# Two attention blocks on one core: the keys' feature map as a power of e on GpSimd

## The chip, the core and the metric

The kernel runs on one core of a Trainium2 chip. The core has TensorE (PE, matmuls), VectorE (DVE), ScalarE (ACT), GpSimd (POOL), and a queue on SyncE (SP) that issues most DMAs. Each engine works through its own list of instructions in order; semaphores tie the lists together. The metric is the device time of one launch in microseconds, as the median of several runs.

## The reference

Two attention blocks, A and B, stand side by side; their outputs are concatenated. Both have a sequence of 2048, a width of 1024 and 32 heads of 32. A is ordinary softmax attention. B goes through four segments of 512 positions. In each it computes causal softmax attention inside the segment and mixes it, by a gate per head, with what it reads from a memory that the earlier segments have written.

```python
phi = lambda t: jnp.where(t > 0, t + 1.0, jnp.exp(t))
for s in range(N):                      # N = 4 segments
    logits = einsum('bhqd,bhkd->bhqk', qs, ks) * scale + mask
    a_dot = einsum('bhqk,bhkd->bhqd', softmax(logits), vs)
    pq = phi(qs)
    num = einsum('bhld,bhde->bhle', pq, M)
    den = einsum('bhld,bhd->bhl', pq, z)[..., None] + 1e-06
    o = g * (num / den) + (1.0 - g) * a_dot
    pk = phi(ks)
    M = M + einsum('bhld,bhle->bhde', pk, vs)
    z = z + pk summed over the segment
```

The feature map phi is what the change is about. It is needed for the keys in segments 0, 1 and 2 (the memory written in the last segment is never read), and for the queries in segments 1, 2 and 3 (the memory is empty in the first).

## The kernel before

The heads are worked on in eight groups of four (4 x 32 = 128 partitions). A's attention is cut into chunks of 256 queries; B's into units, one for each segment s and group j. Both give the same stream: TensorE computes a block of scores into PSUM, ScalarE takes its exponential in pieces of up to 1536 columns (L772) and writes it as P, and TensorE multiplies P with V (L821) and with ones (L827, the softmax's denominator). Where a piece of B lies on the diagonal, GpSimd masks P with an affine_select (L784) before TensorE may use it. VectorE divides and stores. Two sets of three PSUM banks alternate between TensorE and ScalarE, so TensorE can be at most one block of scores ahead.

Everything else is filled in around that stream: projections of keys, queries and values (L449; results are copied out of PSUM by VectorE, L971, L1140 and L1153), output projections (L1250), and B's memory. All of these jobs share one PSUM bank (`X_BANKS`). After each key or query projection GpSimd squares the result (`square`, L977); the squares give a bound on the scores, which is the bias of the exponential.

The order of instructions on every engine is fixed when the program is built. The class `Prog` holds a list of operations, each with an engine, a planned duration, a key (roughly the planned time at which it is wanted) and its reads and writes. `schedule` plays the engines forward with these planned durations. Whenever an engine is free, it takes, among the operations whose inputs are ready, the one with the smallest key; an operation is not held back until its key. TensorE has a rule of its own (`pick`) that puts blocks of scores first and jobs in the gaps. On the chip the engines then follow exactly these lists. The planned durations are `n / rate / 1000 + fixed` us, with `rate` 0.96 for VectorE, 1.2 for ScalarE, 1.2 for GpSimd and 0.5 for GpSimd's squares; the fixed part is 0.12, 0.142 and 0.15 us.

B's memory has three jobs for each segment and group. `job_phi` (L1166) makes the feature map in the tile `PKQ_B`, of which there are two (`j % 2`); each has a key half (index 0) and a query half (index 1). It computes phi(t) as min(exp(t), 1) + max(t, 0): the exponential on ScalarE (L1174) for both halves in one instruction of 1024 columns where both are needed, of 512 columns otherwise; the min on VectorE in place (L1176); the max and sum on VectorE (L1179), one instruction for each half, which for the keys also adds up z. `job_mem` (L1183) reads the memory with the query half. `job_M` (L1205) takes the key halves of two groups, transposes them with eight DMAs from SP's queue (L1215) and adds their product with V to the memory. Its key is `M_AT = 14` us behind the unit's start, while `job_phi` lies in the four us ahead of that start.

The constants are set at the beginning by a chain of GpSimd instructions (`plan_constants`, L624), all of which go through one resource, `r_c`.

Of the kernel before, what the change touches and what calls it, by code (L numbers as in the profile page):

```python
# [5 lines left out]
dt = mybir.dt  # L6
ACT = mybir.ActivationFunctionType
ALU = mybir.AluOpType
AX = mybir.AxisListType

P = 128
# [6 lines left out]
L = 512  # L18
# [10 lines left out]
        (7, 6), (7, 7))  # L29
CHUNKS = [(g, c) for g in range(6) for c in range(8)] + list(PAIR)  # L30
BIAS0 = 16
B_FIRST, B_STEP, B_GAP = 9.0, 1.35, 2.5
B_STEP3 = 1.2

# [20 lines left out]
def holds(rs, *tag):  # L55
    for r in rs:
        assert r.tag == tag, (r.tag, tag)


def mark(rs, *tag):  # L60
    for r in rs:
        r.tag = tag
# [77 lines left out]
MARGIN = 1.5  # L140
# [4 lines left out]
XR = 6  # L145
XC = 0
M_AT = 14.0


class Prog:  # L150
# [266 lines left out]
class _Kernel:  # L417
# [7 lines left out]
    def sb(self, name, shape, dtype=dt.bfloat16):  # L425
        return self.es.enter_context(self.nc.sbuf_tensor(name, shape, dtype))
# [65 lines left out]
    def alloc(self):  # L492
        nc = self.nc
        sb = self.sb
# [67 lines left out]
        self.gc = sb("gc", [P, 4, 8], dt.float32)  # L562
        self.r_g = Res()
        self.warm = sb("warm", [P, 2], dt.float32)
        self.cols = sb("cols", [P, 64], dt.float32)
        self.dg = sb("dg", [P, 2, P], dt.float32)
        self.r_dg = Res()
# [56 lines left out]
    def plan_constants(self):  # L624
        c = self.r_c
        k0 = -100.0

        def pool1(f, n=128):
            self.item(k0, lambda key, f=f, n=n: self.pool(f, n, key, (c,), (c,)))
        pool1(lambda e: e.memset(self.warm[:, :], 0.0), 2)  # L630
        self.item(k0, lambda key: self.act(lambda e: e.activation(self.warm[:, :], self.warm[:, :], ACT.Exp), 1500, key,
                                           (c,), (c,)))
        pool1(lambda e: e.memset(self.identf[:, :], 0.0))
        pool1(lambda e: e.affine_select(self.identf[:, :], self.identf[:, :], pattern=[[-1, P]],
                                        compare_op=ALU.not_equal, fill=1.0, base=0, channel_multiplier=1))
        pool1(lambda e: e.memset(self.onesf[:, :], 1.0))
        pool1(lambda e: e.memset(self.onesb[:, :], 1.0), 32)

        pool1(lambda e: e.memset(self.blk32[:, :], 1.0), 32)
        for r in range(4):  # L640
            rows = slice(32 * r, 32 * r + 32)
            pool1(lambda e, rows=rows, r=r: e.affine_select(
                self.blk32[rows, :], self.blk32[rows, :], pattern=[[1, 32]], compare_op=ALU.is_ge, fill=0.0,
                base=-8 * r, channel_multiplier=0), 32)
            pool1(lambda e, rows=rows, r=r: e.affine_select(
                self.blk32[rows, :], self.blk32[rows, :], pattern=[[-1, 32]], compare_op=ALU.is_ge, fill=0.0,
                base=8 * r + 7, channel_multiplier=0), 32)
        pool1(lambda e: e.memset(self.maskbd[:, :], 1.0))
        for r in range(4):
            rows = slice(32 * r, 32 * r + 32)  # L650
            pool1(lambda e, rows=rows, r=r: e.affine_select(
                self.maskbd[rows, :], self.maskbd[rows, :], pattern=[[1, P]], compare_op=ALU.is_ge, fill=0.0,
                base=-32 * r, channel_multiplier=0))
            pool1(lambda e, rows=rows, r=r: e.affine_select(
                self.maskbd[rows, :], self.maskbd[rows, :], pattern=[[-1, P]], compare_op=ALU.is_ge, fill=0.0,
                base=32 * r + 31, channel_multiplier=0))


    def tiles_att_A(self, g, c, part=None):
# [4 lines left out]
        for t in range(lo, hi):  # L664
# [3 lines left out]
            for h in range(4):  # L668
                tiles.append(dict(unit=("A", g, c), kind="A", g=g, c=c, h=h, w=512, pieces=pieces, set=key, part=part, pv=pv,
                                  bias=BIAS0 if part == 0 else g % 2))  # L670
        return tiles
# [326 lines left out]
    def guard_A0(self, key):  # L998
        col = self.guard_cols(key, self.sqA[(0, 0)] + self.sqA[(0, 1)], 512)
        self.guard_end(key + 0.2, [self.col0, col], 2, [0], halves=True)  # L1000
        rb, r0 = self.r_bias[0], self.r_bias[BIAS0]
        x = self.act(lambda e: e.activation(self.f0[:, :], self.bias[:, BIAS0:BIAS0 + 1], ACT.Exp, bias=self.bias[:, 0:1],
                                            scale=-1.0), 1, key + 1.0, [rb, r0], [self.r_f0])
# [33 lines left out]
    def plan_prologue(self):  # L1037
# [19 lines left out]
        def half0(key):  # L1057
# [20 lines left out]
            self.col0 = self.guard_cols(key, sq, 512)  # L1078
            self.guard_end(key, [self.col0], 2, [BIAS0])
        self.item(-50.0, half0)  # L1080
# [83 lines left out]
        self.sqB.setdefault((s, j), []).append(self.square("B", dst, self.r_KQB[j][kq], key + 1.5))  # L1164

    def job_phi(self, s, j, key):  # L1166
        a, b = (0 if s < 3 else 1), (2 if s > 0 else 1)
        n = (b - a) * L
        holds(self.r_KQB[j], "KQ", s, j)
        mark(self.r_PKQ[j % 2], "P", s, j)  # L1170
        PKQ, rp = self.PKQ[j % 2], self.r_PKQ[j % 2]
        src = self.KQB[:, j, a:b, :]
        rs = [self.r_KQB[j][k] for k in range(a, b)]
        x = self.act(lambda e: e.activation(PKQ[:, a:b, :], src, ACT.Exp), n, key, rs, rp[a:b], fixed=0.19)  # L1174
        x.margin = MARGIN
        self.dve(lambda e: e.tensor_scalar(PKQ[:, a:b, :], PKQ[:, a:b, :], 1.0, None, ALU.min), n / 4, key, rp[a:b], rp[a:b])  # L1176
        for k in range(a, b):
            kw = dict(accum_out=self.zs[:, j:j + 1]) if k == 0 else {}
            self.dve(lambda e, k=k, kw=kw: e.scalar_tensor_tensor(out=PKQ[:, k, :], in0=self.KQB[:, j, k, :], scalar=0.0,  # L1179
                                                                  in1=PKQ[:, k, :], op0=ALU.max, op1=ALU.add, **kw), L,  # L1180
                     key + 0.5, [self.r_KQB[j][k], rp[k]], [rp[k]] + ([self.r_zs[j]] if k == 0 else []))

    def job_mem(self, s, j, key):  # L1183
        holds(self.r_PKQ[j % 2], "P", s, j)
# [129 lines left out]
    def plan_jobs(self):  # L1314
# [34 lines left out]
        for s in range(NSEG):  # L1349
# [31 lines left out]
            for j in range(8):  # L1381
# [4 lines left out]
                if s < 3:  # L1386
                    if j % 2 == 1:
                        self.item(SB[j] + M_AT, lambda key, s=s, j=j: self.job_M(s, j - 1, key))
        for k in range(8):
# [70 lines left out]
```

## Time and profile before

| what | value |
|---|---|
| median of 3 runs | 1219.09 us (1216.64 to 1220.8) |
| the profiled execution | 1215.55 us, of it the span 1213.8 us |
| granted TensorE clock | 0.993 |
| ScalarE, exponentials of scores (L772) | 827 instructions, 1147.0 us busy |
| ScalarE, feature map (L1174) | 16 of 1024 columns, mean 1246 ns; 16 of 512, mean 860 ns |
| VectorE, min of the feature map (L1176) | 16 of 1024, mean 502 ns; 16 of 512, mean 331 ns |
| VectorE, max and sum (L1179) | 48 of 512, mean 786 ns |
| GpSimd, squares (L977) | 124 of 512, 1046 and 1049 ns |
| GpSimd, masks (L784) | 64 of 768, mean 865 ns; 32 of 384, 552 ns; 32 of 128, 357 ns |
| SP, transposes of the feature map (L1215) | 96, median 1233 ns |

A group's mean duration is that of single instructions, and neighbours on ScalarE overlap: the 827 exponentials have a larger sum of durations than the busy time. The span is the time from the first to the last instruction; some 1.75 us of the profiled execution lie outside it.

### The profile page before, as it was taken

How to read it: one execution, taken by the hardware profiler on the slowest of the kernel's cores; microseconds unless marked ns; L12 is line 12 of the kernel's file. 1: busy time of each engine (PE TensorE's matmuls, PEld its weight loads, DVE VectorE, ACT ScalarE, POOL GpSimd, SP SyncE). 2: the span in 40 equal slices, each digit the busy share in tenths (PEclk: the TensorE clock that was granted, in tenths of full speed). 3: DMA queues.
4: the chain of work that ended last, by engine and by line, in shares of the span. 5: the costliest groups of instructions: out<-in, count | busy, mean ns of one | idle time of the engine just before them, and what ended most of it. 6: DMA issues, size and time to landing. Idle time of an engine off the chain costs nothing.

```text
span 1213.8 us, 52835 instructions
## 1 busy us (share of the span) xinstructions
PE 1128.2 (93%) x24712; PEld 544.3 (45%) x24712; DVE 550.1 (45%) x1241; ACT 1166.5 (96%) x870; POOL 216.0 (18%) x279
## 2 busy tenths in 40 slices
PE   6889999999999989998999999999999999899998
PEld 4444444464444445534444444454444444434443
DVE  1234244434352545546443555564535555543222
ACT  3879999999999999999999999999999999999995
POOL 1112131312230211122120221312102231010000
PEclk9989999999999999999999999999999999999999
DMA  9632222303111222202311122201112410001001
GB/s 177 163 78 53 76 60 46 72 20 68 39 41 39 70 49 41 68 19 53 75 24 44 39 52 47 57 25 44 55 46 63 139 33 12 24 25 33 32 29 36
DMA packets 166619, 65.67 MB, mean 54 GB/s; under 512 B 136192, under 2 KB 163584, under 8 KB 166400
## 3 DMA queue, kind: packets, MB, share of 16 engines
q1 hardware_dynamic: 164032, 61.51, 20.8%
q8 instruction: 193, 3.16, 1.1%
q10 hardware_dynamic: 2368, 0.79, 0.3%
q14 instruction: 26, 0.21, 0.1%
HBM read 39.00 MB, written 11.73 MB: 42 GB/s over the span
## 4 chain that ended last, share of the span: by engine, by line
ACT 76%; PE 15%; DVE 4%; issue 3%; SPq 1%; DMA 0%; POOL 0%; DVEq 0%; ACTq 0%
ACT P L772 75%; PE ps L449 8%; PE ps L757 3%; PE ps L821 2%; PE ps L827 2%; ACT PKQ_B L1174 1%; SPq L1050 1%; DVE T L845 1%; DVE PKQ_B L1179 1%; DMA Wv_A<-in_A_wqkv_dram 0%; DVE KQ_A L971 0%; DVE T L854 0%; DVE KQ_B L971 0%; DVE PKQ_B L1176 0%; DVE OT_B L1200 0%
## 5 line engine op out<-in xcount | busy, mean ns | idle before, releaser
L772 ACT ACTIVATE P<-ps,bias 128x1536 bf16<-128x1536 f32 (+3 forms) x827 | 1147.0, 1672 | 16.3 <-PE ps L757 13.3
L827 PE MATMUL ps<-P,onesb 128*32 128x256 bf16 (+1 forms) x4864 | 299.6, 271 | 0.0
L757 PE MATMUL ps<-KQ_A 32*128 32x256 bf16 x4096 | 276.5, 274 | 20.1 <-ACT P L772 16.9
L821 PE MATMUL ps<-P,V_A 128*32 128x256 bf16 x4096 | 259.9, 277 | 10.4 <-ACT P L772 8.9
L757 PEld LDWEIGHTS ps<-KQ_A 32*128 32x128 bf16 x4096 | 80.6, 92 | 240.1 <-ACT P L772 135.2
L449 PE MATMUL ps<-xT_A,W_A 128*32 128x512 bf16 x2048 | 146.8, 388 | 12.7 <-DMA xT_A<-in_A_x_dram 7.3
L821 PEld LDWEIGHTS ps<-P,V_A 128*32 128x32 bf16 x4096 | 109.0, 96 | 82.1 <-issue 41.1
L449 PE MATMUL ps<-xT_B,W_B 128*32 128x512 bf16 x2048 | 142.0, 381 | 4.1 <-DVE cols L994 1.4
L827 PEld LDWEIGHTS ps<-P,onesb 128*32 128x32 bf16 x4864 | 130.6, 97 | 25.7
L784 POOL TENSOR_SCALAR_AFFINE_SELECT P<-P 128x768 bf16<-128x768 bf16 (+2 forms) x128 | 81.5, 660 | 254.7 <-ACT P L772 254.6
L977 POOL TENSOR_TENSOR sqB<-KQ_B 128x512 bf16<-128x512 bf16 x64 | 67.0, 1046 | 319.6 <-DVE KQ_B L971 296.3
L977 POOL TENSOR_TENSOR sqA<-KQ_A 128x512 bf16<-128x512 bf16 x60 | 63.0, 1049 | 298.7 <-DVE KQ_A L971 218.4
L1250 DVE CAST outsb<-ps 128x512 bf16<-128x512 f32 x62 | 42.9, 691 | 144.2 <-PE ps L449 144.1
L845 DVE STREAM_TRANSPOSE T<-ps 128x256 f32<-128x256 f32 (+1 forms) x148 | 72.4, 489 | 65.7 <-PE ps L827 51.5
L971 DVE CAST KQ_B<-ps 128x512 bf16<-128x512 f32 x64 | 44.1, 690 | 124.2 <-PE ps L449 121.9
L971 DVE CAST KQ_A<-ps 128x512 bf16<-128x512 f32 x60 | 41.5, 691 | 119.8 <-PE ps L449 117.8
L449 PE MATMUL ps<-Wv_A,xT_A 128*32 128x256 bf16 x2048 | 73.4, 278 | 9.9 <-issue 6.7
L854 DVE STREAM_TRANSPOSE T<-rc 128x256 f32<-128x256 f32 (+1 forms) x152 | 73.3, 484 | 4.0
L449 PEld LDWEIGHTS ps<-xT_A,W_A 128*32 128x32 bf16 x2048 | 44.9, 97 | 64.8 <-issue 31.4
L449 PE MATMUL ps<-Wv_B,xT_B 128*32 128x512 bf16 x1024 | 70.5, 382 | 2.5 <-DVE cols L994 0.7
L449 PE MATMUL ps<-Wo_B,OT_B 128*32 128x512 bf16 x1024 | 69.6, 382 | 0.8 <-DVE KQ_B L971 0.6
L449 PEld LDWEIGHTS ps<-xT_B,W_B 128*32 128x32 bf16 x2048 | 45.5, 95 | 52.2 <-issue 24.5
(81 smaller groups left out, 744.7 us busy)
## 6 DMA issues: line engine op xcount, KB each, us to landing
Wv_B<-in_B_wv_dram SPq DMA_DIRECT2D x8, 1024.0 KB, 5.5
W_B<-in_B_wk_dram SPq DMA_DIRECT2D x32, 256.0 KB, 3.1
W_B<-in_B_wq_dram SPq DMA_DIRECT2D x32, 256.0 KB, 3.0
out_dram<-outsb SPq DMA_DIRECT2D x62, 128.0 KB, 1.9
W_A<-in_A_wqkv_dram SPq DMA_DIRECT2D x14, 256.0 KB, 3.5
ot_a_scratch<-OTst SPq DMA_DIRECT2D x51, 64.0 KB, 1.8
xT_A<-ot_a_scratch SPq DMA_DIRECT2D x6, 512.0 KB, 8.2
Wv_A<-in_A_wqkv_dram SPq DMA_DIRECT2D x4, 512.0 KB, 5.1
```

The lines of the kernel that those rows point to most:

```text
L449: ins = e.matmul(out[r], w[:, r], x, start=start, stop=stop, tile_position=(0, 32 * t), skip_group_check=True)
L757: ins = e.matmul(out, kap, qap, start=st, stop=True, tile_position=(32 * h, 0), skip_group_check=True)
L772: a = self.act(lambda e: e.activation(dst, src, ACT.Exp, bias=self.bias[:, bc:bc + 1], scale=SCALE), cols, key, res + [self.r_bias[bc]], [rP])
L784: self.pool(lambda e, v=v, pat=pat: e.affine_select(v, v, pattern=pat, compare_op=ALU.is_ge, fill=0.0, base=0, channel_multiplier=-1), (m ...
L821: ins = e.matmul(self.ps[32 * h:32 * h + 32, 512 * obk + q0:512 * obk + q0 + nq], vt[:, c0 + 32 * h:c0 + 32 * h + 32], Pt[:, b, off:off + nq],
L827: ins = e.matmul(self.ps[32 * h:32 * h + 32, lcol + q0:lcol + q0 + nq], self.onesb[:, 0:32], Pt[:, b, off:off + nq], start=False, stop=las ...
L845: self.dve(lambda e: e.transpose(T1[:, 0:n], src), n, key, rsrc, [r1])
L854: self.dve(lambda e: e.transpose(T2[:, 0:n].rearrange("p (b r) -> p b r", r=32), bc), n, key, [rr], [r2])
L971: self.dve(lambda e: e.tensor_copy(dst, out), ncol, key + 1.0, [self.bank[b]], rdst)
L977: self.pool(lambda e: e.tensor_tensor(sq[:, :], src, src, ALU.mult), 512, key, [rsrc], [rs], rate=0.5)
L1050: self.dma(lambda e, i=i, h=h: e.dma_start(self.xT[:, i, 1024 * h:1024 * h + 1024], xa[1024 * h:1024 * h + 1024, P * i:P * i + P], transpo ...
L1250: self.dve(lambda e: e.tensor_copy(ob[:, :], self.ps[:, 512 * b:512 * b + 512]), 512, key + 1.0, [self.bank[b]], [ro])
```

## The change

A constant e is kept in a new tile, `euler`, one float32 for each partition, set by one more GpSimd memset among the constants. In `job_phi` the two halves are separated. The query half stays as it was, with an exponential of 512 columns on ScalarE. The key half is now computed as e to the power of min(t, 0): VectorE takes the min of the keys with 0 (from `KQ_B` straight into `PKQ_B`), then GpSimd raises e to that power in place, in two instructions of 256 elements per partition, with e broadcast along the row. The final max and sum on VectorE is the same, but the key half's gets a key 6 us behind the job's in place of 0.5 us. The plan's duration of a power is 256 / 0.2 / 1000 + 0.15 us.

```diff
+EULER = 2.718281828459045
+POW_N, POW_RATE = 256, 0.2
...
+        self.euler = sb("euler", [P, 1], dt.float32)
...
+        pool1(lambda e: e.memset(self.euler[:, :], EULER), 1)
...
     def job_phi(self, s, j, key):
-        a, b = (0 if s < 3 else 1), (2 if s > 0 else 1)
-        n = (b - a) * L
...
-        src = self.KQB[:, j, a:b, :]
-        rs = [self.r_KQB[j][k] for k in range(a, b)]
-        x = self.act(lambda e: e.activation(PKQ[:, a:b, :], src, ACT.Exp), n, key, rs, rp[a:b], fixed=0.19)
-        x.margin = MARGIN
-        self.dve(lambda e: e.tensor_scalar(PKQ[:, a:b, :], PKQ[:, a:b, :], 1.0, None, ALU.min), n / 4, key, rp[a:b], rp[a:b])
-        for k in range(a, b):
+        src, rs = self.KQB[:, j, :, :], self.r_KQB[j]
+        if s < 3:
+            self.dve(lambda e: e.tensor_scalar(PKQ[:, 0, :], src[:, 0, :], 0.0, None, ALU.min), L / 4, key, [rs[0]], [rp[0]])
+            for h in range(0, L, POW_N):
+                u = PKQ[:, 0, h:h + POW_N]
+                base = self.euler[:, 0:1].to_broadcast([P, POW_N])
+                self.pool(lambda e, u=u, base=base: e.tensor_tensor(u, base, u, ALU.pow), POW_N, key, [rp[0], self.r_c], [rp[0]],
+                          rate=POW_RATE)
+        if s > 0:
+            x = self.act(lambda e: e.activation(PKQ[:, 1, :], src[:, 1, :], ACT.Exp), L, key, [rs[1]], [rp[1]], fixed=0.19)
+            x.margin = MARGIN
+            self.dve(lambda e: e.tensor_scalar(PKQ[:, 1, :], PKQ[:, 1, :], 1.0, None, ALU.min), L / 4, key, [rp[1]], [rp[1]])
+        for k in range(0 if s < 3 else 1, 2 if s > 0 else 1):
             kw = dict(accum_out=self.zs[:, j:j + 1]) if k == 0 else {}
...
-                     key + 0.5, [self.r_KQB[j][k], rp[k]], [rp[k]] + ([self.r_zs[j]] if k == 0 else []))
+                     key + (6.0 if k == 0 else 0.5), [rs[k], rp[k]], [rp[k]] + ([self.r_zs[j]] if k == 0 else []))
```

In the changed kernel job_phi's other lines and the jobs around it stand as they were, and so do the rule by which `schedule` orders the instructions and the planned durations of all that was there.

More of the change, by code (lines that the diff above doesn't have):

```diff
@@ L1171, in job_phi @@
         PKQ, rp = self.PKQ[j % 2], self.r_PKQ[j % 2]
-        src = self.KQB[:, j, a:b, :]
-        rs = [self.r_KQB[j][k] for k in range(a, b)]
-        x = self.act(lambda e: e.activation(PKQ[:, a:b, :], src, ACT.Exp), n, key, rs, rp[a:b], fixed=0.19)
-        x.margin = MARGIN
-        self.dve(lambda e: e.tensor_scalar(PKQ[:, a:b, :], PKQ[:, a:b, :], 1.0, None, ALU.min), n / 4, key, rp[a:b], rp[a:b])
-        for k in range(a, b):
+        src, rs = self.KQB[:, j, :, :], self.r_KQB[j]
[11 more added lines that the diff above has]
+        for k in range(0 if s < 3 else 1, 2 if s > 0 else 1):
             kw = dict(accum_out=self.zs[:, j:j + 1]) if k == 0 else {}
-            self.dve(lambda e, k=k, kw=kw: e.scalar_tensor_tensor(out=PKQ[:, k, :], in0=self.KQB[:, j, k, :], scalar=0.0,
-                                                                  in1=PKQ[:, k, :], op0=ALU.max, op1=ALU.add, **kw), L,
-                     key + 0.5, [self.r_KQB[j][k], rp[k]], [rp[k]] + ([self.r_zs[j]] if k == 0 else []))
+            self.dve(lambda e, k=k, kw=kw: e.scalar_tensor_tensor(out=PKQ[:, k, :], in0=src[:, k, :], scalar=0.0, in1=PKQ[:, k, :],
+                                                                  op0=ALU.max, op1=ALU.add, **kw), L,
+                     key + (6.0 if k == 0 else 0.5), [rs[k], rp[k]], [rp[k]] + ([self.r_zs[j]] if k == 0 else []))
     def job_mem(self, s, j, key):
```

## The prediction

> **What bounds the kernel now.** I read the page's first part, then the busy time by stretches, who ScalarE waited for, and ScalarE's timeline.
>
> ```profile
> PE 1128.2 (93%) x24712; PEld 544.3 (45%) x24712; DVE 550.1 (45%) x1241; ACT 1166.5 (96%) x870; POOL 216.0 (18%) x279
> ...
> 120.00:240.00 120.00, 114.80 (x2440) 52.61 (x2434) 49.39 (x114) 119.81 (x90) 28.10 (x31) 1.00 0.27 64
> 480.00:600.00 120.00, 111.91 (x2523) 56.62 (x2515) 67.57 (x159) 117.36 (x89) 25.61 (x32) 0.97 0.17 42
> 960.00:1080.00 120.00, 110.28 (x2326) 50.79 (x2330) 65.83 (x152) 120.00 (x92) 20.88 (x28) 1.00 0.14 43
> ...
> ACT P L772 <- PE ps L757: 13.3, 11, 6.1
> ACT KQ_A L1075 <- PE ps L449: 13.1, 1, 13.1
> ACT outsb L1252 <- PE ps L449: 10.7, 2, 7.8
> ```
>
> In the stretches the columns after the length are PE, PEld, DVE, ACT and POOL. ScalarE is busy 956.2 of the 960 us from 120 to 1080 us (eight stretches, three shown), so only 3.8 us are idle there; its other idle time lies in the start and the last output rows. TensorE is busy 904.1 of the same 960 us: 56 us free. ScalarE sets the end, and TensorE is a close second. The end should therefore move with ScalarE's work until something makes TensorE late.
>
> **What the change takes from ScalarE.** The duration of a ScalarE row is not its price, because one instruction starts before the last has drained. The price is the step from its start to the next start:
>
> ```profile
> 235.26 0.88 ACT L1174 ACTIVATE PKQ_B<-KQ_B 128x512 bf16<-128x512 bf16 x1
> 235.78 4.65 ACT L772 ACTIVATE P<-ps,bias 128x1536 bf16<-128x1536 f32 x3
> ...
> 422.09 1.19 ACT L1174 ACTIVATE PKQ_B<-KQ_B 128x1024 bf16<-128x1024 bf16 x1
> 423.04 5.97 ACT L772 ACTIVATE P<-ps,bias 128x1536 bf16<-128x1536 f32 x4
> ```
>
> 235.78 - 235.26 = 0.52 us for 512 columns, 423.04 - 422.09 = 0.95 us for 1024. Segment 0 loses its eight 512s: 8 x 0.52 = 4.2 us. Segments 1 and 2 turn sixteen 1024s into 512s: 16 x (0.95 - 0.52) = 6.9 us. Segment 3 has queries only and keeps its eight. Together **11.0 us**, on the path that sets the end. (By durations, 1.25 and 0.86 us, it would be 13.1 us, which is too much.)
>
> **What it puts on GpSimd.** 24 (segment, group) pairs get two powers of 256 elements: 48 new instructions. No row shows a power, so its cost is bounded.
>
> ```profile
> L977 POOL TENSOR_TENSOR sqB<-KQ_B 128x512 bf16<-128x512 bf16 x64 | 67.0, 1046 | 319.6 <-DVE KQ_B L971 296.3
> ...
> L784 POOL TENSOR_SCALAR_AFFINE_SELECT P<-P 128x768 bf16<-128x768 bf16 x64 | 55.3, 865 | 254.7 <-ACT P L772 254.6
> ...
> L852 DVE RECIPROCAL rc<-T 128x8 f32<-128x8 f32 x128 | 25.6, 200 | 3.3
> ...
> L850 DVE RECIPROCAL rc<-rc 128x16 f32<-128x16 f32 x24 | 5.9, 245 | 0.6
> ...
> L1106 DVE TENSOR_TENSOR sqA<-KQ_A 128x512 bf16<-128x512 bf16 x4 | 1.4, 416 | 0.0
> ```
>
> Below, a power is no cheaper than a square: 1046 / 2 = 0.52 us. Above, the nearest row of a function that takes several steps is VectorE's reciprocal: eight elements more cost 45 ns, 5.6 ns each; the same square takes GpSimd 1046 and VectorE 416 ns, a factor of 2.5; 256 x 5.6 x 2.5 = 3.6 us. Between them stands the plan's own figure in the diff, 256 / 0.2 + 150 ns = **1.43 us**, and I take it, because the plan's other GpSimd figures lie near their rows: 1.17 against 1.05 us for the square, 0.79 against 0.87 us for the 768-wide select. That is 48 x 1.43 = 68.6 us more on GpSimd: 216 becomes 285 us of some 1205, far from a bound by sum.
>
> The Trainium skill (GPSIMD Engine Reference, Elementwise — side-by-side cycle accounting) says that data-dependent branching on this engine costs about 12 cycles per element; at its 1.2 GHz a power that branches would be an estimated 2.6 us, inside the slow rival below. No run here shows yet whether it branches.
>
> **What the power delays.** Three things queue behind it or need it.
>
> GpSimd's own queue: the selects that mask P come in bursts, and the PV matmuls need them. TensorE's wait for them is now 3.4 us in all, at most 0.7 us each, although 124 squares of 1.05 us (130 us) stand in that queue already. Powers add half as much again; by that share it is some 2 us more of TensorE waits, from its 56 us.
>
> VectorE: the min of the key half now runs ahead of the power without waiting for ScalarE, and the sum (L1179) waits for the second power. What stands behind that sum in VectorE's queue, above all the casts that free the single projection bank, waits too, and TensorE for them. The order is laid out with 1.43 us, so a power as long as planned costs nothing here; a longer one makes the sum late by twice the excess. Splitting the min gives 48 of the 512 form for 16 + 16: 48 x 0.33 - 13.3 = 2.6 us on an engine busy 45%. The slack is seen in these:
>
> ```profile
> L1179 DVE SCALAR_TENSOR_TENSOR PKQ_B<-KQ_B,PKQ_B x48: 640/692/1436, 173.4 to 1073.0; 128x512 bf16<-128x512 bf16 x48
> ...
> L1176 DVE TENSOR_SCALAR PKQ_B<-PKQ_B x32: 282/418/1217, 172.8 to 1072.0; 128x512 bf16<-128x512 bf16 x16, 128x1024 bf16<-128x1024 bf16 x16
> ```
>
> The sum's longest is 1.44 against a median of 0.69 us; those sums that lie mostly beside a GpSimd instruction are the long ones (eleven, median 1.19 us). Delays of up to 0.75 us happen now while ScalarE idles 3.8 us in 960. So about 0.75 us of lateness is free.
>
> SP's queue: the eight transposes of a pair (L1215, 1.23 us each) wait for the sum. Their product is used in the next segment: the same group's feature maps start at 171.9 and at 354.1 us, 180 us apart, so even a late one costs nothing there; other loads behind them would be late by the same excess only.
>
> The constant's memset (0.1 us, like the 98 to 101 ns rows) lies in the constants' chain, before anything that the first matmuls' loads need: nothing; 0.3 us with its hand-over if that cover were gone.
>
> **Sum.** -11.0 for ScalarE; plus 4 us for new waits, which is ScalarE's present idle time there doubled (bounds: 0 if TensorE's 56 us absorb all, 8 if idle time triples, since the cover shrinks by 11 us). -7.0 us. The profiled execution took 1215.55 us (span 1213.8, 1.75 around it), which gives 1208.5; the median of the runs is 1219.09, 3.5 us above, so the forecast for the timed runs is **1212 us**, 0.6% faster. With the bounds 0 to 8 us and the runs' own spread of 2 us below and above, 1206 to 1218; as a likely core 1207 to 1215.
>
> **Rivals.**
>
> *The power is much slower than planned.* At 2.5 us, the middle between 1.43 and the upper bound, the sum is late by 2 x 1.07 = 2.14 us, 1.4 beyond what is free. VectorE is busy 45% of the time, so that is about the chance that something is held: 24 x 1.4 x 0.45 = 15 us, 1212 + 15 = 1227. At 3.6 us: 24 x (4.34 - 0.75) x 0.45 = 39 us, 1251. Even with before it stands at a power of about 2.1 us (24 x 0.65 x 0.45 = 7). For: the plan's figure may be a guess, and a power is several steps. Against: the other figures are right.
>
> *VectorE is held by the powers at 1.43 us already.* An operation like the sum that meets a GpSimd instruction is stretched (above), and a power is longer than a square. If each pair meets two such operations for the whole 1.43 us, 48 x (1.43 - 0.75) x 0.45 = 15 us: 1227, slower. It decides once more than about 23 of the 48 powers do so (7 us / (0.68 x 0.45)). Against: at random, powers fill 6% of the time, and of some 200 such operations 12 would be hit, by half a power each: 8 us on an idle engine.
> The Trainium skill (SBUF — State Buffer, SBUF: two separate sides) has this as an exclusive lock: a VectorE operation with two SBUF inputs or in a 2-port mode and a GpSimd operation shut each other out for the whole instruction. The stretched sums above agree (1.19 against 0.69 us); by its rule alone each meeting costs up to a whole power.
>
> *TensorE is the bound.* If its 56 free us are not usable (its ends are modelled), ScalarE's 11 us turn into idle time, and the time stays at 1219. For: 110 to 115 of every 120 us. Against: ScalarE hardly ever waits for it.
>
> **Chances.** Forecast 0.60; slow power 0.16; held VectorE 0.12; TensorE the bound 0.12. A measurement of this kernel tells about 0.3% (3.7 us) from no change. Faster by more: 0.60; within it: 0.12; slower: 0.16 + 0.12 = 0.28. The range must reach the slower cases until two in ten are left out: 1205 (all 11 us and the fastest runs) to 1236 (a power near 2.9 us).
>
> **What will show it.** ScalarE's busy time about 11 us lower, with L1174's sixteen 1024 rows gone and 24 of 512 left; the power's row near 1.4 us and GpSimd near 285 us; ScalarE's idle time from 120 to 1080 us below 12 us; VectorE's waits for the power short. I am wrong if the power's row is above 2.1 us, if VectorE waits for it by tens of us, or if ScalarE's waits for L757 grow by the 11 us it was given.

## The result

The changed kernel takes 3168.41 us (median of 4 runs, 3165.83 to 3171.54) against 1217.87 us for the kernel before in the same series: a ratio of 2.605 (95% interval 2.597 to 2.614). The profiled execution took 3170.28 us, of it the span 3168.5 us.

First the page's first part, three rows of its slices, the chain that ended last, and the group of the new instruction, all of the changed kernel:

```profile
PE 1191.9 (38%) x24712; PEld 560.8 (18%) x24712; DVE 557.1 (18%) x1257; ACT 1164.7 (37%) x862; POOL 2189.3 (69%) x328
...
ACT  5413009006006030445031060050290060199998
POOL 1797992994985979555969939959649959712100
PEclk9756559558558565777565585575695585599999
...
POOL 60%; PE 16%; ACT 14%; issue 3%; SPq 3%; DVE 2%; DMA 1%; DVEq 0%; ACTq 0%
...
L1181 POOL TENSOR_TENSOR PKQ_B<-euler,PKQ_B 128x256 bf16<-128x256 f32 x48 | 1973.0, 41117 | 61.5 <-DVE PKQ_B L1177 60.9
```

One power of 256 elements takes **41.1 us**, not 1.43. GpSimd's 2189 us are the 216 of before and 1973 of powers. ScalarE, which was busy in nearly every slice before, now works mostly where GpSimd does not: until the powers end, its row and GpSimd's are nearly each other's negatives. TensorE's granted clock shows 5 tenths in the slices in which ScalarE's row shows 0, and 9 at the end.

GpSimd is busy for 69% of the span, so its sum alone (2189 us) does not set the end. Who waited for whom in the changed kernel (the waiting engine, tile and line; what ended the wait; total us, times, longest):

```profile
DVE PKQ_B L1189 <- POOL PKQ_B L1181: 1901.6, 24, 122.2
ACT P L776 <- PE ps L761: 1793.6, 71, 121.2
...
DVE PKQ_B L1177 <- DMA PKt_B<-PKQ_B: 52.1, 10, 8.8
```

Four powers, two for each of two groups, show in the timelines of GpSimd, VectorE, TensorE and ScalarE how the first becomes the second (start, length, instruction, and in brackets the idle time before it):

```profile
556.17 82.21 POOL L1181 TENSOR_TENSOR PKQ_B<-euler,PKQ_B 128x256 bf16<-128x256 f32 x2 [9.14 <-DVE PKQ_B L1177]
639.34 82.20 POOL L1181 TENSOR_TENSOR PKQ_B<-euler,PKQ_B 128x256 bf16<-128x256 f32 x2
...
558.42 0.69 DVE L975 CAST KQ_A<-ps 128x512 bf16<-128x512 f32 x1 [1.49 <-PE ps L451]
680.49 1.09 DVE L1189 SCALAR_TENSOR_TENSOR PKQ_B<-KQ_B,PKQ_B 128x512 bf16<-128x512 bf16 x1 [121.37 <-POOL PKQ_B L1181]
681.52 0.68 DVE L975 CAST KQ_A<-ps 128x512 bf16<-128x512 f32 x1
721.57 1.52 DVE L1189 SCALAR_TENSOR_TENSOR PKQ_B<-KQ_B,PKQ_B 128x512 bf16<-128x512 bf16 x1 [39.38 <-POOL PKQ_B L1181]
...
682.34 0.62 PE L991 MATMUL ps<-sqA,blk 128*32 128x512 bf16 x4 [116.81 <-DVE KQ_A L975]
...
561.33 5.15 ACT L776 ACTIVATE P<-ps,bias 128x1536 bf16<-128x1536 f32 x4 [0.83 <-PE ps L761]
683.57 1.54 ACT L776 ACTIVATE P<-ps,bias 128x1536 bf16<-128x1536 f32 x1 [117.09 <-PE ps L761]
```

The sum L1189 stands on VectorE where the plan expects the power to be done. The powers of the two groups alternate in GpSimd's list, so the first sum needs the third power, which ends 41.1 us behind 639.34. VectorE stands in front of this sum for 121 us, and in front of the second sum for another 39 us. The cast behind the first sum (681.52), which frees the projection bank, is late; TensorE's next matmul (L991) waits 117 us for it with the scores behind it in TensorE's list, and ScalarE gets its next scores after 117 us. VectorE waits for the powers 24 times, 79 us on average.

The second line of waits, L1177 for a DMA, is small here. It turns out below to be a loss of its own that would have made the change slower even with a cheap power.

### The profile page after: what moved, and what is told of

The parts are those of the page before. It is cut to its first block, busy times and chain, and to the rows that moved or that the text cites. A ratio compares the mean times of both kernels' runs of the same rounds, so it can differ in the third digit from the quotient of the medians.

```text
span 3168.5 us, 52797 instructions
## 1 busy us (share of the span) xinstructions
PE 1191.9 (38%) x24712; PEld 560.8 (18%) x24712; DVE 557.1 (18%) x1257; ACT 1164.7 (37%) x862; POOL 2189.3 (69%) x328
## 4 chain that ended last, share of the span: by engine, by line
POOL 60%; PE 16%; ACT 14%; issue 3%; SPq 3%; DVE 2%; DMA 1%; DVEq 0%; ACTq 0%
POOL PKQ_B L1181 60%; ACT P L776 14%; PE ps L451 8%; PE ps L761 3%; SPq L1225 3%; PE ps L825 2%; PE ps L831 2%; DMA PKt_B<-PKQ_B 1%; DVE PKQ_B L1189 1%; SPq L1054 0%; DVE T L849 0%; DVE KQ_B L975 0%; DVE T L858 0%; POOL sqB L981 0%; DVE V_B L1157 0%
## 5 line engine op out<-in xcount | busy, mean ns | idle before, releaser
L1181 POOL TENSOR_TENSOR PKQ_B<-euler,PKQ_B 128x256 bf16<-128x256 f32 x48 | 1973.0, 41117 | 61.5 <-DVE PKQ_B L1177 60.9
L825 PE MATMUL ps<-P,V_A 128*32 128x256 bf16 x4096 | 275.7, 289 | 488.1 <-DVE OTst L900 322.7
L1189 DVE SCALAR_TENSOR_TENSOR PKQ_B<-KQ_B,PKQ_B 128x512 bf16<-128x512 bf16 x48 | 47.3, 985 | 1902.2 <-POOL PKQ_B L1181 1901.6
L831 PE MATMUL ps<-P,onesb 128*32 128x256 bf16 (+1 forms) x4864 | 316.0, 282 | 0.0
L451 PE MATMUL ps<-xT_B,W_B 128*32 128x512 bf16 x2048 | 150.6, 400 | 430.6 <-DVE KQ_B L975 307.9
L761 PE MATMUL ps<-KQ_A 32*128 32x256 bf16 x4096 | 287.4, 283 | 24.2 <-ACT P L776 20.8
L451 PE MATMUL ps<-xT_A,W_A 128*32 128x512 bf16 x2048 | 154.4, 410 | 122.7 <-DVE cols L998 77.4
L451 PE MATMUL ps<-Wo_B,OT_B 128*32 128x512 bf16 x1024 | 78.9, 417 | 160.3 <-DVE outsb L1260 156.7
L451 PE MATMUL ps<-PKQ_B,Mb 128*32 128x512 bf16 x96 | 10.2, 414 | 233.8 <-DVE V_A L1144 156.4
L991 PE MATMUL ps<-sqA,blk 128*32 128x512 bf16 x64 | 7.2, 441 | 235.3 <-DVE KQ_A L975 234.6
```

Of the source, the lines that this page charges most:

```text
L451: ins = e.matmul(out[r], w[:, r], x, start=start, stop=stop, tile_position=(0, 32 * t), skip_group_check=True)
L761: ins = e.matmul(out, kap, qap, start=st, stop=True, tile_position=(32 * h, 0), skip_group_check=True)
L825: ins = e.matmul(self.ps[32 * h:32 * h + 32, 512 * obk + q0:512 * obk + q0 + nq], vt[:, c0 + 32 * h:c0 + 32 * h + 32], Pt[:, b, off:off + nq],
L831: ins = e.matmul(self.ps[32 * h:32 * h + 32, lcol + q0:lcol + q0 + nq], self.onesb[:, 0:32], Pt[:, b, off:off + nq], start=False, stop=las ...
L991: ins = e.matmul(self.ps[32 * c:32 * c + 32, 512 * b:512 * b + 512], self.blk32[:, :], sq[:, :], start=True, stop=True, tile_position=(0, ...
L1181: self.pool(lambda e, u=u, base=base: e.tensor_tensor(u, base, u, ALU.pow), POW_N, key, [rp[0], self.r_c], [rp[0]], rate=POW_RATE)
```

## The experiments

Ratios are to the kernel before, on the same chip, with 95% intervals.

**The power by itself.** A kernel with nothing but single GpSimd instructions, each waited for, and VectorE's sums and mins beside them:

```diff
+done(g.tensor_tensor(o[:, 0:512], b(ef, 512), xh[:, 0:512], ALU.pow))
...
+done(g.tensor_tensor(o[0:1, 0:256], b(ef, 256, 1), xh[0:1, 0:256], ALU.pow))
```

> The power by itself, nothing of the two blocks computed (the output is a memset of zeros). On GpSimd one after the other: an add and a mult of 256 elements, powers of 512, 256, 128, 64 and 16 elements with exponent -0.5, powers of 256 with exponents 0, -0.0025, -3 and 2, with base 1, with a bf16 base that is not broadcast, with float32 in and out, powers of 256 on 16, 4 and 1 partitions, a float32 square and two tensor_scalars of 256. VectorE runs 24 sums (scalar_tensor_tensor, two SBUF inputs) and 24 mins beside the powers, after 8 sums without. Theory (the price is per element and for each partition lane in turn): 256 take 41 us, 512 82 us, 128 21 us, the same for all exponents to within some per cent, and on 16 partitions still 41 us, on 4 about a quarter, on 1 about a sixteenth. Rival (price of the values: small exponents take a slow branch): exponents 0 and -3 differ by more than 20 per cent. Rival (price of the operands: broadcast float32 base with bf16): the bf16 base or all-float32 form takes under 30 us. Rival (a fixed price of each instruction, such as code that is loaded): 16 elements take over 10 us. On VectorE: if a power holds the shared port for its whole length, a sum beside it takes up to 41 us; if not, at most 1.1 us, as in the changed kernel's trace.

Its groups (line, engine, operation, tiles, shapes, count; busy us, mean ns):

```profile
L66 POOL TENSOR_TENSOR o<-ef,xh 128x512 bf16<-128x512 f32 x1 | 82.3, 82258 | 0.1
L76 POOL TENSOR_TENSOR o<-eb,xh 128x256 bf16<-128x256 bf16 x1 | 41.2, 41170 | 0.1
L71 POOL TENSOR_TENSOR o<-ef,x 128x256 bf16<-128x256 f32 x1 | 41.1, 41125 | 0.1
...
L73 POOL TENSOR_TENSOR o<-ef,x 128x256 bf16<-128x256 f32 x1 | 41.1, 41115 | 0.1
...
L77 POOL TENSOR_TENSOR of<-ef,xf 128x256 f32<-128x256 f32 x1 | 41.1, 41115 | 0.1
...
L80 POOL TENSOR_TENSOR o<-ef,xh 1x256 bf16<-1x256 f32 x1 | 41.1, 41105 | 0.1
...
L43 DVE SCALAR_TENSOR_TENSOR vc<-va,vb 128x512 bf16<-128x512 bf16 x24 | 16.6, 693 | 0.8
...
L70 POOL TENSOR_TENSOR o<-ef,xh 128x16 bf16<-128x16 f32 x1 | 2.9, 2895 | 0.1
...
L81 POOL TENSOR_TENSOR of<-xf 128x256 f32<-128x256 f32 x1 | 0.6, 612 | 0.1
```

From 16 to 512 elements the time grows by (82258 - 2895) / 496 = 160 ns per element on a fixed 0.3 us. L71 has exponents of 0, L73 of -3, L76 a bf16 base that is not broadcast, L77 float32 throughout: the price is the same. The rivals of values, operands and a fixed price fall. One partition (L80) costs as much as 128, so my own guess that it would scale with the partitions falls too. VectorE's 24 sums (L43) run from 13.1 to 30.6 us, beside the power of 82 us that starts at 8.3, and take 693 ns: the power does not hold VectorE for its length.

**The right price in the plan.**

```diff
-POW_N, POW_RATE = 256, 0.2
+POW_N, POW_RATE = 256, 0.00625
```

> The changed kernel with the plan's duration of a power set to 256 / 0.00625 + 150 ns = 41.1 us, what the profile shows. Theory (the loss is VectorE parked in front of each late pair of powers, 24 x 79 us = 1900 us, and only because the order was laid out with 1.43 us): VectorE's wait for L1189 falls from 1902 us to under 300 us, and the time goes from 3168 to what GpSimd needs, 48 x 41.1 + 216 us + its start of 107 us, 2300 us or somewhat more. Rival (the maps are needed in the stream anyhow, so the order does not matter): the time stays within 5 per cent of 3168 us.

2655.62 us in one run: better by 513 us, not as good as 2300. The waits of this kernel:

```profile
ACT P L776 <- PE ps L831: 1327.8, 56, 65.1
DVE PKQ_B L1189 <- POOL PKQ_B L1181: 1069.1, 23, 69.5
PE ps L825 <- POOL P L788: 1043.5, 51, 37.3
```

GpSimd is now the bound while it has powers to do: busy 2128 of the 2180 us from 120 to 2300. The masks stand behind the powers in its queue, and TensorE waits 1043 us for them. The powers are over by 2300 us, and 354 us of the stream are left behind them, which my 2300 had not counted. VectorE's wait was to fall under 300 us and fell to 1069. So some 500 us of the loss, by this one run, were the order's blindness. The powers' own sum of 1973 us stays whatever the order, and is more than the whole kernel before.

**A cheap operation in the power's place.**

```diff
-e.tensor_tensor(u, base, u, ALU.pow)
+e.tensor_tensor(u, base, u, ALU.add)
```

> The changed kernel with an add of e in place of the power, same shapes and same plan (the keys' map then is e + min(t, 0) + max(t, 0), not e^min(t, 0) + max(t, 0)). The operation takes some 0.55 us, less than the planned 1.43 us. Theory (only the price of the power was wrong): ScalarE is 11 us lighter, new waits take 0 to 8 us back, 0.990 to 0.998 of before, 1207 to 1215 us by the first median. Rival (VectorE is held by GpSimd's new instructions, or TensorE is the bound): ratio 1.000 or above.

1263.70 us, ratio 1.040 (1.037 to 1.043). The rival's side: with an operation of 0.63 us, less than half of the planned 1.43, the changed kernel is still 4% slower than before. The price of the power was not all that was wrong.

**Three adds for each power.**

```diff
-self.pool(lambda e, u=u, base=base: e.tensor_tensor(u, base, u, ALU.pow), ..., rate=POW_RATE)
+for r in range(3):
+    self.pool(lambda e, u=u, base=base: e.tensor_tensor(u, base, u, ALU.add), ..., rate=0.783)
```

> As the one before, but each power is replaced by three adds of 256 elements, planned at 0.48 us each and likely to take some 0.6 us each, 1.8 us for what was planned at 1.43 us (the keys' map is 3e + min(t, 0) + max(t, 0)). Theory (a GpSimd price near the planned one leaves the gain): 0.990 to 0.998 of before. Rival (GpSimd at that price holds VectorE or the masks): 1.000 or above, with VectorE's waits for L1181 of 10 us or more.

1264.58 us, 1.042 (1.039 to 1.044), with three adds of 0.62 us: 1.87 us in place of 0.63, and the same time. Both signs of the rival are there, a ratio above 1 and over 10 us of waits: VectorE waited 12.4 us for the last of the adds (7 times, up to 3.6). But in add_cheap, which is just as slow, it waited 3.9 us. So GpSimd's price up to 1.87 us is not what costs the 4%. The waits of add_cheap name another candidate:

```profile
DVE PKQ_B L1177 <- DMA PKt_B<-PKQ_B: 52.5, 10, 8.1
...
ACT P L776 <- PE ps L761: 57.0, 29, 8.2
```

The min L1177 writes into the key half of `PKQ_B`, which the transposes of the group two before (L1215 before, L1225 now) must have read. Ten times it stands on VectorE before they have landed, and ScalarE's wait for scores is 57.0 us where it was 13.3.

**A truer plan of the transposes, in add_cheap.**

```diff
-self.sm_PKt, key, self.r_PKt, reads=rp, issue=0.7, lat=3.0)
+self.sm_PKt, key, self.r_PKt, reads=rp, issue=1.25, lat=3.0)
```

> add_cheap (an add of e in place of the power) with one number of the plan changed: a transpose of the feature map is planned at 1.25 us of SP's queue in place of 0.7 us; the profile shows 1.23 us. In add_cheap the min of the keys' map, which may overwrite PKQ_B only when the transposes of two groups earlier have landed, waits for them 52.5 us on VectorE (10 times, up to 8.1 us). Theory (the 4 per cent of add_cheap are these waits: the map no longer waits for its turn on ScalarE, so the plan pulls it forward to the moment at which it believes the transposes done, and it believes them done too early): L1177's wait for the DMA falls under 10 us and the ratio to before is 0.99 to 1.00. Rival (GpSimd's adds themselves hold VectorE or the masks): the ratio stays above 1.03.

1218.24 us, 1.0024 (1.0007 to 1.0041). VectorE's wait for the DMA fell from 52.5 to 9.7 us and 38 of the 40 thousandths went with it. But it is just above 1.00: ScalarE is idle 12.3 us from 120 to 1080 us where it was 3.8, and one of the three waits that were left took 7.9 us at a stroke.

**The same plan in the kernel before.** The same one-line edit.

> The kernel before with the same change of the planned transposes, 1.25 in place of 0.7 us, as a control. Theory: nothing waits for these transposes there that is in a hurry, since the exponential of the map takes its turn on ScalarE by its key; ratio 0.997 to 1.003. Rival (the truer plan is a gain by itself): below 0.997, and then add_dma is to be compared with this.

1217.71 us, 1.0016 (0.9999 to 1.0032): no gain and no clear loss, as the control was to show.

**The min held back.** add_cheap once more, with transposes planned at 0.7 us as they were:

```diff
-self.dve(lambda e: e.tensor_scalar(PKQ[:, 0, :], src[:, 0, :], 0.0, None, ALU.min), ...)
+x = self.dve(lambda e: e.tensor_scalar(PKQ[:, 0, :], src[:, 0, :], 0.0, None, ALU.min), ...)
+x.margin = 10.0
```

> add_cheap (an add of e in place of the power, transposes planned at 0.7 us as in the kernel before) with the min of the keys' map held back in the plan: a margin of 10 us behind the moment at which its inputs are believed ready. Theory (the 4 per cent are the min's early place on VectorE, and what add_dma still lacked are the waits that were left, 9.7 us for the transposes and what they held): L1177's wait for the DMA is 0, ScalarE's idle time from 120 to 1080 us falls from add_dma's 12.3 towards before's 3.8 us, and the ratio is 0.992 to 0.999. Rival (TensorE is the bound once ScalarE is lighter): the waits are gone but the ratio stays at 1.000 to 1.005, as in add_dma.

1208.14 us, **0.9947** (0.9927 to 0.9967). Here is a gain of the size that I had forecast for the change, 6.7 us, but with an add of 0.62 us in the power's place. The first row of the page and two of its waits:

```profile
PE 1125.5 (93%) x24712; PEld 545.6 (45%) x24712; DVE 553.8 (46%) x1257; ACT 1156.1 (96%) x862; POOL 248.2 (21%) x328
...
ACT P L776 <- PE ps L761: 11.1, 8, 3.2
...
DVE PKQ_B L1177 <- DMA PKt_B<-PKQ_B: 5.9, 2, 4.3
```

ScalarE is busy 1156.1 against 1166.5 us. Its idle time from 120 to 1080 us is 7.1 us, 3.2 more than before. The wait for the DMA did not vanish, as I had expected, but it is 5.9 us in place of 52.5. TensorE, 93% busy, follows: that rival falls.

**The power with the min held back.** The same edit in the changed kernel itself.

> The changed kernel, power and all, with the same margin of 10 us for the min of the keys' map. Theory (in the changed kernel the late power hides the early min: VectorE stands in front of the sum anyhow): the time changes by less than 3 per cent of 3168 us. Rival (the early place of the min makes a large part of the loss, since VectorE is stopped in worse moments): below 2900 us.

3112.00 us in one run: 56 us or 1.8% less, within the 3% that I expected, but not for my reason: the late power does not hide the early min. In size the two losses add up. The early min costs 1263.7 - 1208.1 = 56 us with the cheap add and 3168.4 - 3112.0 = 56 us with the power; the power in the add's place costs 3168.4 - 1263.7 = 1905 us with the early min and 3112.0 - 1208.1 = 1904 us without. These are differences between runs on different chips, where the kernel before took 1214 to 1218 us, and one of them is a single run, so the agreement to 1 us is partly luck. VectorE's wait for the powers changed as well, from 1901.6 to 1825.7 us, so that the 56 us are the same loss both times is not shown.

**A version that computes the map and gains.** The exponential on GpSimd without a power: with m the key clamped to [-64, 0], ((1 + m/64)^2 + 1) / 2, squared six times in float32, in halves of 256.

```diff
...
+self.pool(lambda e, u=u: e.tensor_scalar(W, u, 1.0 / 64.0, 1.0, ALU.mult, ALU.add), ...)
+self.pool(lambda e: e.tensor_tensor(W, W, W, ALU.mult), ...)
+self.pool(lambda e: e.tensor_scalar(W, W, 1.0, 0.5, ALU.add, ALU.mult), ...)
+for _ in range(5):
+    self.pool(lambda e: e.tensor_tensor(W, W, W, ALU.mult), ...)
+self.pool(lambda e, u=u: e.tensor_tensor(u, W, W, ALU.mult), ...)
```

> A candidate that computes the reference: the keys' exponential on GpSimd without the power, as ((1 + m/64)^2 + 1) / 2 to the 64th by six squarings in float32, m the key clamped to [-64, 0], in halves of 256 elements: 18 short instructions of 0.4 and 0.6 us (measured alone: 0.404 and 0.612 us) for a pair, some 10 to 12 us on GpSimd, with the transposes planned at 1.25 us and a ring of three output tiles in place of four, for room. Theory (11 us of ScalarE are to be had if GpSimd's instructions are short, known to the plan, and not pulled into a wait): 0.990 to 0.998 of before, GpSimd some 480 us busy. Rival (GpSimd's share holds the masks and VectorE): 1.00 or above.

1219.60 us, 1.0028 (1.0006 to 1.0050): the rival's side, with 10.2 us of VectorE's waits for the transposes.

> sq_keys (the keys' exponential by squarings on GpSimd, transposes planned at 1.25 us) with the same margin of 10 us for its clamp on VectorE. Theory: VectorE's waits for the DMA (10.2 us) go, the ratio falls from 1.003 to 0.993 to 0.999. Rival (TensorE is the bound): 1.000 to 1.005.

1211.50 us, **0.9968** (0.9954 to 0.9983): faster than the kernel before, and than the changed one, with GpSimd 470 us busy. VectorE's waits for the transposes are gone from its list.

**The queries' half as well.** sq_keys with the second half done in the same way.

> The same for the queries' half too, so that ScalarE does no feature map at all: 33.7 us of rows, 23.5 us of its time by the steps between starts (16 x 0.52 + 16 x 0.95). Theory: 0.982 to 0.995 of before if TensorE can follow; GpSimd some 750 us busy. Rival (TensorE, with 56 us free before, becomes the bound, or the queries' map comes late for the memory's read): no better than sq_keys.

1265.56 us, 1.041 (1.039 to 1.044). ScalarE has no map left to compute, and waits:

```profile
ACT P L776 <- PE ps L831: 55.2, 16, 12.8
ACT P L776 <- PE ps L761: 28.0, 13, 9.3
...
DVE PKQ_B L1194 <- POOL PKQ_B L1180: 25.3, 13, 4.1
```

GpSimd is busy 718 us here, VectorE waits for it 25.3 us and for the transposes 17.4 us. Which of these makes TensorE late was not separated, and the margin was not tried in this version.

## Why the prediction was wrong

**The price of the power** is the term that failed: I bounded it by 0.52 and 3.6 us and took 1.43; it is 41.1. The lower bound held. The upper one was too low by a factor of 11: I took VectorE's reciprocal as the nearest function of several steps and multiplied it by the ratio of the engines at a square, but a row of another operation on another engine says nothing of how this engine computes a power. The choice between the ends rested on the plan's figure, because its other GpSimd figures were near their rows. Those could be compared with rows; this one had none. The estimate of 2.6 us for a power that branches was low by a factor of 16.

**The mechanism of the slow rival was right, and its size follows from the price.** A sum late by twice the excess, with 0.75 us free, is 24 x (2 x (41.1 - 1.43) - 0.75) = 1886 us if every stall reaches ScalarE; the power in the add's place measured 1904 and 1905 us. The factor 0.45, the chance that something stands behind a sum, was meant for stalls of a microsecond, and no run tested it there. With stalls of 80 us the measured loss leaves no room for it: something stood behind nearly all of them.

**The transposes: "even a late one costs nothing there"** was the second wrong step, and it would have decided alone: 56 us, against a forecast gain of 7. I asked who uses the transposes' product (180 us later) and not who reuses their source. The exponential had taken its turn on ScalarE by its key, and in the plan a margin of 1.5 us (`MARGIN`) held it back behind its inputs; in the trace of before ScalarE never waits for the transposes. The min on VectorE has no such turn, and the change gave it no margin. VectorE is often idle (busy 45% before), and an operation is not held back until its key, so the maps move forward. The first one's first instruction starts at 171.9 us before and at 100.4 us in add_cheap (start of the first and the last behind the durations):

```profile
L1174 ACT ACTIVATE PKQ_B<-KQ_B x32: 684/1044/1407, 171.9 to 1071.2; 128x512 bf16<-128x512 bf16 x16, 128x1024 bf16<-128x1024 bf16 x16
...
L1177 DVE TENSOR_SCALAR PKQ_B<-KQ_B x24: 248/294/593, 100.4 to 836.7; 128x512 bf16<-128x512 bf16 x24
```

Where its keys are ready, what stops a min in the plan is the buffer: it is put at the moment at which the plan believes the transposes landed, with 0.7 us for each where the profile of before showed 1.23. Both numbers were to be had.

**What held.** ScalarE's 11.0 us: its busy time fell by 10.4 us in add_margin. The new waits of 4 us: its idle time in the middle grew by 3.2 us. Together -7.0 forecast, -6.7 measured (4.0 to 8.9 by the interval), once the two losses are taken away. That the two are so close is partly luck: the 4 us were a doubling of the present idle time and no mechanism gave them, and an add of 0.62 us is not the power of 1.43 us of the forecast. The chance of 0.60 was for the change as it stood, and there the two other steps decide.

**The other rivals.** VectorE held by GpSimd's instructions through a port: tripling them (add_three against add_cheap) changed nothing, and sums beside a power took 693 ns. By the Trainium skill (SBUF — State Buffer, SBUF: two separate sides) the shut-out lasts for the whole instruction; the trace of micro_pow agrees in kind for short instructions (two sums that met the add and the mult took 984 ns in place of 691) and for the first 2 us of the power (1410 ns), but not for the 20 us after that, in which sums beside the power took 691 to 693 ns; later in it no sum ran. TensorE as the bound: add_margin gained, so it was not, at 93% busy.

## What to carry to other kernels

An operation that no row of a profile shows is to be measured alone before a kernel is built on it; a figure in a plan is not a measurement, and a far row of another engine is no upper bound. When work moves from a busy engine to an idle one, it also loses the place that the busy queue gave it: look at what it may now overtake, above all the last reader of the buffer that it writes, and compare the plan's durations of that reader with the profile's. Where a change has several effects, a cheap stand-in for the disputed operation shows whether the rest would have worked.

## What the runs showed of the hardware

A power on GpSimd costs 160 ns per element of the free dimension, for all exponents from -3 to 2, both types, and all numbers of partitions that micro_pow tried (41.1 us for 256 elements on 1 and on 128 partitions). A float32 square of 256 elements, an element times itself, takes 0.61 us there, a tensor_scalar with two operations 0.40 us; fourteen and four of these make an exponential of 512 columns, 14 x 0.612 + 4 x 0.404 = 10.2 us by sum, against 82 us for two powers. (In sq_margin GpSimd is busy 470 - 216 = 254 us more than before, 10.6 us for each of 24 maps.) VectorE's two-input sums ran at 693 ns beside a power, from 2 to 22 us behind its start. Why the power is so slow inside, these runs do not show.
